# Spreading U of units 4 to 7 by TensorE, and calling for half of w1 and w2 three steps later

## The chip, the cores and the metric

The kernel runs on one core of a Trainium2 chip. The core has five engines that run beside each other and wait for one another by semaphores: TensorE (PE, matmuls; its weight loads are listed as PEld), VectorE (DVE), ScalarE (ACT), GpSimd (POOL) and SyncE (SP), which here only issues transfers. Sixteen DMA engines move data between HBM and the on-chip memory. The metric is device time in microseconds (us), the median of several executions; lower is better.

## The reference

The program computes an mLSTM cell over 4 batches, 8 heads, 768 positions and head size 40, and feeds the result to a multiplicative feed-forward block. Cut to what matters:

```python
for t in range(S):
    m_new = np.maximum(f_gate[:, :, t] + m, i_gate[:, :, t])
    f_stab = np.exp(f_gate[:, :, t] + m - m_new)
    i_stab = np.exp(i_gate[:, :, t] - m_new)
    C = f_stab * C + i_stab * outer(v_t, k_t)          # per batch and head
    n = f_stab * n + i_stab * k_t
    y[:, :, t] = sigmoid(o_gate_t) * (C @ q_t) / max(|n . q_t|, 1)
# (B, H, S, D) -> (B*S, H*D), 3072 tokens of 320
a = x @ w1                    # 320 x 1024
b = x @ w2                    # 320 x 1024
out = ((a * b) @ w3) @ w_out  # 1024 x 1024, 1024 x 320
```

The weights arrive as 64-bit floats. The kernel loads their words as 32-bit integers and makes 32-bit floats of them on the chip.

## The kernel before

The recurrence over time is done in blocks. A unit is 128 positions of one batch with all 8 heads; there are 24 units (6 blocks of positions by 4 batches), unit n being block `c = n // 4` of batch `b = n % 4`. One step s of the main loop finishes unit s - 1 and begins unit s, and does some matmuls of the feed-forward block beside it. The weight of one position in another is the exponential of a sum of two terms. One of them, U, is the same for all source positions, so the row of U that belongs to a head has to be spread over 64 partitions. For units 0 to 3 TensorE does that: a column of the identity matrix, broadcast, picks the row. For all later units U was written to HBM at the start and is read back with a broadcast over partitions, two transfers of 128 KB a unit.

```python
B, L, P, NU = 4, 64, 128, 24            # batches, half unit, unit, units
...
def load_u(n):                           # U of unit n from HBM, broadcast over 64 partitions
    c, b = divmod(n, B)
    src = U_d[2 * c:2 * c + 2, b * H:(b + 1) * H, :].rearrange("x h t -> x (h t)")
    for x in range(2):
        nc.sync.dma_start(out=weights_tile(n)[halves[x]].rearrange("p h t -> p (h t)"),
                          in_=src[x:x + 1].to_broadcast([L, H * L]))
...
def spread(n):                           # U of unit n by TensorE, into one PSUM bank
    ub = mps([P, H, L], "ub")
    for h in range(H):
        r = n % B * H + h
        for x in range(2):
            mm(ub[halves[x], h, :], ident[0:RG, r:r + 1].to_broadcast([RG, L]), U[:, x * L:(x + 1) * L])
    return ub

def weights(n):
    c, b = divmod(n, B)
    src = weights_tile(n) if c else spread(n)
    pw = weights_tile(n)
    for h in range(H):
        nc.scalar.activation(out=pw[:, h, :], in_=src[:, h, :], func=AF.Exp, bias=aT[:, c, b * H + h:b * H + h + 1])
    for r in halves:                     # the causal mask, on GpSimd
        nc.gpsimd.affine_select(out=pw[r], in_=pw[r], compare_op=OP.is_ge, fill=0.0, base=0,
                                pattern=[[0, H], [1, L]], channel_multiplier=-1)

def turn(n):                             # k and q of units 0 to 9 transposed by TensorE
    ...
    for src, dst, name in ((kbuf[n % NB], kT_t, "kT"), (qbuf[n % NBQ], qT_t, "qT")):
        pt = mps([128, NP, P], "pt")
        for p in range(NP):
            transpose(pt[:, p, :], src[:, 2 * p:2 * p + 2, :].rearrange("p a b -> p (a b)"))
        dst[n] = sb.tile([128, NP, P], FP, name=name, tag=name)
        nc.scalar.copy(out=dst[n], in_=pt)

def weighted(n):                         # vw: v times the input weight, on GpSimd
    ...
```

`mps` hands out one of four PSUM banks, which the transposes (pt, px), U (ub) and the up-products (pa, pb) share in the first part of the kernel. [...]

A weight tile goes through three hands: `fetch` issues its transfer (a tile of w1 or w2 is 128 rows of 4 KB, 512 KB), `scale_next` scales its two words on ScalarE, and `convert` puts them together on VectorE. The tiles of w1 and w2 are called w0 to w9 here: w0 to w4 hold the first half of the columns (the fifth tile the rest of the rows, in both), w5 to w9 the second half. Then come eight tiles of w_out and sixteen of w3. The first transfers, and the plan by steps:

```python
load(0, slice(0, 2))                     # k and q of unit 0
fetch("w12", 0, 0)
load(0, slice(2, 3))                     # v
fetch("w12", 1, 0)
load_o(0)
fetch("w12", 2, 0)
idle += [w3o_words[:, i * CW:(i + 1) * CW] for i in range(2)]
fetch("w12", 3, 0)
fetch("w12", 4, 0)
load(1)                                  # k, q, v of unit 1
load_o(1)
...                                      # the gates' scans on DVE, then
turn(0)
gate_cols(a, aT, nc.scalar.copy)
scale_next(True)                         # w0
scale_next(True)                         # w1
convert()
nc.scalar.activation(out=w, in_=w, func=AF.Exp)
weights(0)
...
scale_next(True)                         # w2
convert()
...
todo = w12[KF * 2 + 1:] + [("wo", ...)] + [("w3", ...)]
n_cvt = [2, 1, 1, 1, 2, 2, 3, 3, 3] + [2] * 7    # conversions in each step
turned, converted, fetched = 0, 2, 2 * KF + 1    # KF is 2

for s in range(len(n_up)):
    if B <= s + 3 < NU:
        load_u(s + 3)
    if s + 2 < NU:
        load(s + 2); load_o(s + 2)
    if 0 < s < B - 1:
        weights(s + 1); out_gate(s)
    if s < NU:
        weighted(s)
        ...
        if 0 < s < N_DVE:
            turn(s)
    ...                                  # x_trans (px): y of an earlier unit turned for the feed-forward
    now = [ups.pop(0) for _ in range(n_up[s])]   # n_up: 1 in steps 4 and 5, 2 in steps 6 to 16
    open_ups = [up(*x) for x in now]     # pa, pb
    ...                                  # up_rest, then the cell: unit s-1 finished, unit s begun (ss, pc)
    if s == 0:
        gate_cols(g, gT, nc.scalar.copy); out_gate(0); scale_next(); weights(1)
    if B - 1 <= s < NU:
        weights(s + 1); out_gate(s)
    for _ in range(n_cvt[s]):
        convert(); converted += 1        # scales first if nothing is scaled
    ...
    while todo and fetched < converted + (2 if s < 2 else 3 if s < ahead - 1 else 4):
        fetch(*todo.pop(0)); fetched += 1
```

The second half of the columns of w1 and w2 is first used by the up-products of step 7.

Of the kernel before, what the change touches and what calls it, by code (L numbers as in the profile page):

```python
# [16 lines left out]
def kernel(  # L17
# [28 lines left out]
    B, H, S, D = q.shape  # L46
    L = 64
    P = 128
    NT = S // L
    NT2 = S // P  # L50
    NU = NT2 * B
# [6 lines left out]
    FO = DFF // P  # L58
    KF = DM // P
# [17 lines left out]
    def mps(shape, name):  # L77
        pool = banks.pop(0)
        banks.append(pool)
        return pool.tile(shape, FP, name=name, tag="m")  # L80
# [10 lines left out]
    def mm(out, lhsT, rhs, start=True, stop=True):  # L91
        in_order(nc.tensor.matmul(out, lhsT=lhsT, rhs=rhs, start=start, stop=stop))  # L92
# [4 lines left out]
    halves = [slice(0, L), slice(L, P)]  # L97
# [3 lines left out]

    NB, NBQ = 4, 3
    N_DVE = 10
    q_all = const.tile([P, NBQ * H * DP], FP, name="q_all")
    qbuf = [q_all[:, i * H * DP:(i + 1) * H * DP].rearrange("p (h d) -> p h d", d=DP) for i in range(NBQ)]
    kbuf = [const.tile([P, H, DP], FP, name=f"kbuf{i}") for i in range(NB)]
    vbuf = [const.tile([P, H, D1], FP, name=f"vbuf{i}") for i in range(NB)]
    ident = const.tile([P, P], FP, name="ident")
# [16 lines left out]
    def load(n, which=slice(0, 3)):  # L125
        for dst, src in ((kbuf[n % NB][:, :, 0:D], k), (qbuf[n % NBQ][:, :, 0:D], q), (vbuf[n % NB][:, :, 0:D], v))[which]:
            if src is not q or n < N_DVE:
                nc.sync.dma_start(out=dst, in_=rows(src, n))  # L128
# [11 lines left out]
    def load_o(n):  # L140
        o_t[n] = io.tile([P, H, D], FP, name="o_in", tag="o_in", bufs=4)
        nc.sync.dma_start(out=o_t[n], in_=rows(o_gate, n))
# [8 lines left out]
    def weights_tile(n):  # L151
        if n not in u_t:
            u_t[n] = io.tile([P, H, L], FP, name="pw", tag="pw", bufs=5)
        return u_t[n]
# [45 lines left out]
    def fetch(kind, i, part):  # L200

        if kind == "w12":
            c0 = part * CW
            if i < 2 * KF:
                wt, src = ((w1, w1_d), (w2, w2_d))[i // KF]
                ko = i % KF
                dst, pieces = wt[:, ko, c0:c0 + CW], [(every, src[ko * 128:(ko + 1) * 128, cols(c0, CW)])]
            else:
                dst, pieces = wr[:, c0:c0 + CW], [(slice(j * REM, (j + 1) * REM), src[KF * P:DM, cols(c0, CW)])
                                                  for j, src in enumerate((w1_d, w2_d))]  # L210
        elif kind == "wo":
            dst, pieces = wo[:, i, :], [(square, wo_d[j * CQ + i * 32:j * CQ + (i + 1) * 32, :])
                                        for j, square in enumerate(squares)]
        else:
            dst, pieces = None, [(square, w3_d[i * 128 + part * 64:i * 128 + (part + 1) * 64, cols(j * CQ, CQ)]
                                  .rearrange("(m r) n -> r m n", m=2)) for j, square in enumerate(squares)]
        pend.append((dst, raw_tile(dst.shape[-1] if dst is not None else CW, pieces), i, part))
# [5 lines left out]
    def scale_next(early=False):  # L223
        scaled.append(pend.pop(0))
        scale(scaled[-1][1], early)
# [36 lines left out]
    def spread(n):  # L262


        ub = mps([P, H, L], "ub")
        for h in range(H):
            r = n % B * H + h
            for x in range(2):
                mm(ub[halves[x], h, :], ident[0:RG, r:r + 1].to_broadcast([RG, L]), U[:, x * L:(x + 1) * L])
        return ub  # L270

    def weights(n):
        c, b = divmod(n, B)
        src = weights_tile(n) if c else spread(n)
        pw = weights_tile(n)
        for h in range(H):
            nc.scalar.activation(out=pw[:, h, :], in_=src[:, h, :], func=AF.Exp, bias=aT[:, c, b * H + h:b * H + h + 1])  # L277
        for r in halves:
            nc.gpsimd.affine_select(out=pw[r], in_=pw[r], compare_op=OP.is_ge, fill=0.0, base=0,  # L279
                                    pattern=[[0, H], [1, L]], channel_multiplier=-1)  # L280
# [161 lines left out]
    RG = GR * BH  # L442
# [19 lines left out]
    load(0, slice(0, 2))  # L462
    fetch("w12", 0, 0)
    load(0, slice(2, 3))
    fetch("w12", 1, 0)
    load_o(0)
    fetch("w12", 2, 0)
    idle += [w3o_words[:, i * CW:(i + 1) * CW] for i in range(2)]
    fetch("w12", 3, 0)
    fetch("w12", 4, 0)  # L470
    load(1)
    load_o(1)

    nc.vector.memset(on, 1.0)
    nc.vector.memset(on.rearrange("p (c t) -> p c t", t=L)[:, :, 0:1], 0.0)
# [221 lines left out]
    n_seven = [0] * 19 + [1] * 12 + [0]  # L697
    n_down = [0] * 17 + [2] * 6 + [1] * 7 + [0, 5]
    w12 = [("w12", i, part) for part in range(2) for i in range(2 * KF + 1)]
    todo = w12[KF * 2 + 1:] + [("wo", i, 0) for i in range(FO)] + [("w3", ko, part) for ko in range(FO) for part in range(2)]  # L700
    n_cvt = [2, 1, 1, 1, 2, 2, 3, 3, 3] + [2] * 7
    pinned, ahead = 32, 9
    behind = ExitStack()
    turned, converted, fetched = 0, 2, 2 * KF + 1

    for s in range(len(n_up)):
        if B <= s + 3 < NU:
            load_u(s + 3)
        if s + 2 < NU:
            load(s + 2)  # L710
            load_o(s + 2)
        if 0 < s < B - 1:
            weights(s + 1)
            out_gate(s)
        if s < NU:
            weighted(s)
            if s >= B:
                decayed(state[s % B][1], state[s % B][0], s, 0)
            if 0 < s < N_DVE:
                turn(s)  # L720
        if NY <= s - 2 < NU:
            send(s - 2)
        elif 0 <= s - 2 < NY:
            twice(s - 2)
        if NY <= s - 2 < NU:
            get_back(s - 2)
        while turned < min(s - 2, NY):
            x_trans(turned)
            turned += 1
        fold()  # L730
        seven = None
        if n_seven[s]:
            seven = up_by_seven(*sevens.pop(0), (lambda i: cell[i // 2][:, i % 2].rearrange("p (i t) -> p i t", i=2)) if s <= NU else
                                lambda i: mps([128, 2, TH], "p67" if i < 2 else "p15"))
            if s <= NU:
                seven[0]()
            seven[1]()
        if seven and s <= NU:
            ffn_out([downs.pop(0) for _ in range(n_down[s])], [cell[1][:, i, 0:DM] for i in range(2)])
        else:  # L740
            for _ in range(n_down[s]):
                ffn_out([downs.pop(0)])
        if seven and s > NU:
            seven[0]()
        now = [ups.pop(0) for _ in range(n_up[s])]
        open_ups = [up(*x) for x in now]
        if len(now) == 1 and turned == s - 2 < NY:
            x_trans(turned)
            turned += 1

        def rest():
            for x in open_ups:
                up_rest(*x)
            if seven:
                seven[2]()

        gated = None
        if s <= NU:
            gated = quarter_work(s, rest)
        else:  # L760
            rest()
        with tc.issue_after(gated.ins) if gated else nullcontext():
            if seven:
                seven[3]()
            if NY <= s - 2 < NU:
                x_turn(s - 2)
            if N_DVE <= s + 1 < NU:
                gated = turn(s + 1)
            if s in (16, 17):
                weight_sums(s - 16)  # L770
            if s - 2 in range(4 * GT - 1, NU, GT):
                token_sums((s - 2) // GT)
        if s == 0:
            gate_cols(g, gT, nc.scalar.copy)
            out_gate(0)
            scale_next()
            weights(1)
        if s == NU:
            cell_psum.close()
            banks.extend([ps_m] * 3 + [ctx.enter_context(tc.tile_pool(name="ps_x", bufs=4, space=bass.MemoryType.PSUM))] * 4)  # L780
        if B - 1 <= s < NU:
            if s + 1 < NU:
                weights(s + 1)
            out_gate(s)
        with tc.issue_after(gated.ins) if N_DVE <= s + 1 < NU else nullcontext():
            for _ in range(n_cvt[s] if s < len(n_cvt) else 0):
                convert()
                converted += 1
        if s >= ahead:
            while pend and len(scaled) < 2:  # L790
                scale_next()
        if N_DVE <= s + 2 < NU:
            load_turned(s + 2)
        while todo and fetched < converted + (2 if s < 2 else 3 if s < ahead - 1 else 4):
            fetch(*todo.pop(0))
            fetched += 1
        if s + 1 == pinned:
            for ins in keep_order(front):
                behind.enter_context(tc.issue_after(ins))
# [30 lines left out]
```

## Time and profile before

| what | value |
|---|---|
| median time of 3 runs | 447.19 us (446.38 to 449.67) |
| span of the profiled execution | 445.8 us |
| PE busy | 423.7 us, 95% of the span |
| PEld busy | 335.5 us, 75% |
| DVE busy | 306.3 us, 69% |
| ACT busy | 149.3 us, 34% |
| POOL busy | 81.7 us, 18% |
| moved by the DMA engines | 52.72 MB, mean 118 GB/s |
| transfers of U (pw<-U_d) | 40 of 128 KB, 3.7 us from issue to landing |

The page of the profile cuts the span into 40 slices of about 11 us; one digit is the busy share of an engine in a slice in tenths, and the line PEclk is the clock that TensorE was granted, in tenths of full speed. Groups of instructions are named by line, engine, operation, and the tiles written and read, as `pw<-U_d`. An answer of the timeline starts with the start and the length of an instruction or a merged row of them, and ends in brackets with the idle time before it and what ended that. A wait for several semaphores is put down to the one that came last.

### The profile page before, as it was taken

The numbers are of one execution on the slowest core, as the hardware profiler recorded it, in microseconds if no ns is written. First come the engines' busy times: TensorE is split into PE (matmuls) and PEld (weight loads), VectorE is DVE, ScalarE is ACT, GpSimd is POOL, SyncE is SP. The second block draws the span as 40 slices with busy tenths as digits, with TensorE's granted clock in tenths as the row PEclk, the third lists the DMA queues.
The fourth block names the chain that finished last, engine by engine and source line by source line (L and its number), as shares of the span: only waits on it lengthen the run. The fifth ranks groups of instructions, "written<-read, shape, count | busy, mean of one in ns | idle before, by whom it ended". The sixth has DMA issues, their size and how long they took to land.

```text
span 445.8 us, 12871 instructions
## 1 busy us (share of the span) xinstructions
PE 423.7 (95%) x5271; PEld 335.5 (75%) x5271; DVE 306.3 (69%) x639; ACT 149.3 (34%) x407; POOL 81.7 (18%) x154
## 2 busy tenths in 40 slices
PE   4768989898999999999999999999999999999997
PEld 3656877787878878787877877778778777777774
DVE  5578387668866976696677949668699776444800
ACT  3766465445752454253212321213211111101110
POOL 3344043233211220222022203202020000000000
PEclk9995899999999999999999999999999999999999
DMA  8999989778988798697366466364111120000001
GB/s 203 182 175 201 200 142 170 172 176 166 205 198 186 147 180 177 161 165 140 83 116 148 102 132 140 76 136 109 50 35 35 39 46 16 15 16 15 1 30 44
DMA packets 136555, 52.72 MB, mean 118 GB/s; under 512 B 109936, under 2 KB 127536, under 8 KB 136496
## 3 DMA queue, kind: packets, MB, share of 16 engines
q1 hardware_dynamic: 132896, 47.87, 53.7%
q10 hardware_dynamic: 3600, 4.03, 2.7%
q8 instruction: 41, 0.67, 0.7%
q14 instruction: 18, 0.15, 0.1%
HBM read 46.07 MB, written 5.80 MB: 116 GB/s over the span
## 4 chain that ended last, share of the span: by engine, by line
PE 80%; DMA 5%; SPq 5%; ACT 3%; DVE 2%; POOL 2%; issue 2%; DVEq 0%; POOLq 0%
PE cell L92 22%; PE pa L92 18%; PE po L92 14%; PE pb L92 12%; PE wp L92 8%; PE p L92 5%; SPq L173 2%; SPq L128 2%; DMA raw<-in_moe_w_dram 2%; DMA o_in<-in_o_gate_dram 1%; DMA kbuf<-in_k_dram 1%; PE px L95 1%; POOL pw L279 1%; ACT pw L277 1%; ACT raw L180 1%
## 5 line engine op out<-in xcount | busy, mean ns | idle before, releaser
L92 PE MATMUL pa<-xT,w 128*128 128x256 f32 x240 | 62.1, 391 | 0.6 <-ACT xT L437 0.6
L92 PE MATMUL po<-w3o,ab 128*128 128x320 f32 x224 | 61.8, 433 | 0.0
L92 PEld LDWEIGHTS po<-w3o,ab 128*128 128x128 f32 x224 | 42.4, 190 | 17.3 <-issue 0.4
L306 POOL TENSOR_TENSOR state<-state,decay 128x164 f32<-128x164 f32 x40 | 19.7, 492 | 182.5 <-DVE den L387 168.2
L92 PEld LDWEIGHTS pa<-xT,w 128*128 128x128 f32 x240 | 45.7, 195 | 8.5 <-ACT xT L437 1.0
L92 PE MATMUL pb<-xT,w 128*128 128x256 f32 x192 | 45.9, 382 | 2.3 <-ACT kT L296 2.3
L583 DVE TENSOR_TENSOR ab<-pb,a_sb 128x512 f32<-128x512 f32 x24 | 16.6, 692 | 43.6 <-ACT a_sb L582 43.6
L279 POOL TENSOR_SCALAR_AFFINE_SELECT pw<-pw 64x512 f32<-64x512 f32 x48 | 34.4, 717 | 52.9 <-ACT pw L277 48.3
L92 PE MATMUL cell<-w3o,ab 128*128 128x320 f32 x160 | 44.0, 432 | 0.0
L92 PEld LDWEIGHTS pb<-xT,w 128*128 128x128 f32 x192 | 36.7, 192 | 8.2 <-ACT kT L296 3.1
L277 ACT ACTIVATE pw<-pw,aT 128x64 f32<-128x64 f32 x160 | 40.2, 336 | 2.8 <-ACT o_sb L685 2.8
L582 ACT ACTIVATE a_sb<-pa 128x512 f32<-128x512 f32 x24 | 14.3, 598 | 76.3 <-PE pb L92 76.3
L92 PEld LDWEIGHTS cell<-w3o,ab 128*128 128x128 f32 x160 | 30.4, 190 | 12.0
L630 DVE SCALAR_TENSOR_TENSOR a_sb<-pa,wo 128x512 f32<-128x512 f32 x12 | 8.3, 692 | 43.2 <-PE pa L92 43.2
L92 PE MATMUL pa<-xT,wr 64*64 64x256 f32 x384 | 36.8, 386 | 0.0
L92 PE MATMUL pb<-xT,wr 64*64 64x256 f32 x384 | 36.2, 379 | 0.0
L92 PE MATMUL wp<-wo,w3T 128*128 128x320 f32 x128 | 35.8, 432 | 0.0
L379 DVE TENSOR_TENSOR h<-cell,h 64x164 f32<-64x164 f32 x96 | 31.3, 326 | 1.8
L92 PEld LDWEIGHTS wp<-wo,w3T 128*128 128x128 f32 x128 | 23.7, 190 | 8.9
L92 PEld LDWEIGHTS pa<-xT,wr 64*64 64x64 f32 x384 | 19.0, 132 | 14.4 <-issue 8.4
L685 ACT COPY o_sb<-po 128x320 f32<-128x320 f32 x14 | 6.0, 427 | 67.4 <-PE po L92 67.4
L92 PEld LDWEIGHTS pb<-xT,wr 64*64 64x64 f32 x384 | 20.2, 133 | 3.0
(128 smaller groups left out, 722.8 us busy)
## 6 DMA issues: line engine op xcount, KB each, us to landing
raw<-in_moe_w_dram SPq DMA_DIRECT2D x64, 128.0 KB, 3.4
pw<-U_d SPq DMA_DIRECT2D x40, 128.0 KB, 3.7
kbuf<-in_k_dram SPq DMA_DIRECT2D x24, 160.0 KB, 4.5
vbuf<-in_v_dram SPq DMA_DIRECT2D x24, 160.0 KB, 5.1
o_in<-in_o_gate_dram SPq DMA_DIRECT2D x24, 160.0 KB, 4.8
out_dram<-o_sb ACTq DMA_DIRECT2D x24, 160.0 KB, 1.8
raw<-in_moe_w_dram SPq DMA_DIRECT2D x7, 512.0 KB, 5.6
raw<-in_moe_w_out_dram SPq DMA_DIRECT2D x32, 80.0 KB, 2.3
```

Source lines behind the costliest of these rows:

```text
L92: in_order(nc.tensor.matmul(out, lhsT=lhsT, rhs=rhs, start=start, stop=stop))
L95: in_order(nc.tensor.transpose(out, in_, ident[0:n, 0:n]))
L128: nc.sync.dma_start(out=dst, in_=rows(src, n))
L173: nc.sync.dma_start(out=dst, in_=src)
L277: nc.scalar.activation(out=pw[:, h, :], in_=src[:, h, :], func=AF.Exp, bias=aT[:, c, b * H + h:b * H + h + 1])
L279: nc.gpsimd.affine_select(out=pw[r], in_=pw[r], compare_op=OP.is_ge, fill=0.0, base=0, pattern=[[0, H], [1, L]], channel_multiplier=-1)
L306: nc.gpsimd.tensor_tensor(out=new, in0=old, op=OP.mult, in1=decay[:, b * NP:(b + 1) * NP, 2 * c + x:2 * c + x + 1] .to_broadcast([P, NP, D1]))
L379: nc.vector.tensor_tensor(out=part, in0=ph[x][halves[e]], in1=part, op=OP.add)
L582: nc.scalar.mul(out=a_sb, in_=pa, mul=UP ** -2)
L583: nc.vector.tensor_tensor(out=ab_t[gr][j][:, fs[0]:fs[-1] + 1, t0:t0 + a_sb.shape[-1]], in0=pb, in1=a_sb, op=OP.mult)
L630: nc.vector.scalar_tensor_tensor(out=out, in0=p, scalar=UP ** -2, in1=q, op0=OP.mult, op1=OP.add)
L685: nc.scalar.copy(out=o_sb, in_=po)
```

## The change

Two things are changed.

- Units 4 to 7, the second block of positions, get U by TensorE as units 0 to 3 do, so 8 transfers of 128 KB are no longer needed. `spread` takes the block's columns of U, which stay on the chip until step 8.
- Of w1 and w2 only three tiles are called for before the main loop. The last two of the first half follow in steps 0 and 1, and the second half in steps 3 to 5, where before it was steps 0 to 4. Conversions move accordingly: 1, 1, 1, 0 in the first four steps where there were 2, 1, 1, 1, and 4 in each of steps 7 and 8 where there were 3. The rows of k, q, v and o of the second unit are called for between the first tiles of words.

The aim is to take transfers out of the first part of the kernel, in which the DMA engines are busy nearly all the time, and to have the rows of the next units arrive sooner.

```diff
+    N_PE = 8
     def spread(n):
+        c, b = divmod(n, B)
         ub = mps([P, H, L], "ub")
         for h in range(H):
-            r = n % B * H + h
+            r = b * H + h
             for x in range(2):
-                mm(ub[halves[x], h, :], ident[...], U[:, x * L:(x + 1) * L])
+                mm(ub[halves[x], h, :], ident[...], U[:, c * P + x * L:c * P + (x + 1) * L])
     def weights(n):
-        src = weights_tile(n) if c else spread(n)
+        src = weights_tile(n) if n >= N_PE else spread(n)
     load(0, slice(0, 2))
     fetch("w12", 0, 0)
     load(0, slice(2, 3))
+    load(1, slice(0, 2))
     fetch("w12", 1, 0)
     load_o(0)
+    load(1, slice(2, 3))
     fetch("w12", 2, 0)
+    load_o(1)
     idle += [w3o_words[:, i * CW:(i + 1) * CW] for i in range(2)]
-    fetch("w12", 3, 0)
-    fetch("w12", 4, 0)
-    load(1)
-    load_o(1)
-    todo = w12[KF * 2 + 1:] + [("wo", ...)] + [("w3", ...)]
-    n_cvt = [2, 1, 1, 1, 2, 2, 3, 3, 3] + [2] * 7
+    todo = w12[3:] + [("wo", ...)] + [("w3", ...)]
+    n_cvt = [1, 1, 1, 0, 2, 2, 3, 4, 4] + [2] * 7
+    n_fetch = [4, 5, 5, 7, 9, 12, 16, 20]
-    turned, converted, fetched = 0, 2, 2 * KF + 1
+    turned, converted, fetched = 0, 2, 3
     for s in range(len(n_up)):
-        if B <= s + 3 < NU:
+        if N_PE <= s + 3 < NU:
             load_u(s + 3)
...
         if s == 0:
             gate_cols(g, gT, nc.scalar.copy)
             out_gate(0)
-            scale_next()
             weights(1)
...
-        while todo and fetched < converted + (2 if s < 2 else 3 if s < ahead - 1 else 4):
+        while todo and fetched < (n_fetch[s] if s < len(n_fetch) else converted + 4):
             fetch(*todo.pop(0))
             fetched += 1
```

Cuts are marked by three dots; line numbers move by one or two.

More of the change, by code (lines that the diff above doesn't have):

```diff
@@ L262, in spread @@
     def spread(n):
+        c, b = divmod(n, B)
         ub = mps([P, H, L], "ub")
         for h in range(H):
-            r = n % B * H + h
+            r = b * H + h
             for x in range(2):
-                mm(ub[halves[x], h, :], ident[0:RG, r:r + 1].to_broadcast([RG, L]), U[:, x * L:(x + 1) * L])
+                mm(ub[halves[x], h, :], ident[0:RG, r:r + 1].to_broadcast([RG, L]), U[:, c * P + x * L:c * P + (x + 1) * L])
         return ub
@@ L699 @@
     w12 = [("w12", i, part) for part in range(2) for i in range(2 * KF + 1)]
-    todo = w12[KF * 2 + 1:] + [("wo", i, 0) for i in range(FO)] + [("w3", ko, part) for ko in range(FO) for part in range(2)]
-    n_cvt = [2, 1, 1, 1, 2, 2, 3, 3, 3] + [2] * 7
+    todo = w12[3:] + [("wo", i, 0) for i in range(FO)] + [("w3", ko, part) for ko in range(FO) for part in range(2)]
+    n_cvt = [1, 1, 1, 0, 2, 2, 3, 4, 4] + [2] * 7
+    n_fetch = [4, 5, 5, 7, 9, 12, 16, 20]
     pinned, ahead = 32, 9
     behind = ExitStack()
-    turned, converted, fetched = 0, 2, 2 * KF + 1
+    turned, converted, fetched = 0, 2, 3
     for s in range(len(n_up)):
-        if B <= s + 3 < NU:
+        if N_PE <= s + 3 < NU:
             load_u(s + 3)
```

## The prediction

> **What bounds the kernel now.** I read the page first: the slices of the span, then the share of each engine. TensorE (PE) is at nine tenths or more from the sixth slice on, and the DMA engines at eight tenths or more through the first nine slices, so two different limits follow each other.
>
> ```profile
> PE   4768989898999999999999999999999999999997
> ...
> PEclk9995899999999999999999999999999999999999
> DMA  8999989778988798697366466364111120000001
> ```
>
> What comes after about 60 us is a full queue on PE: a microsecond lost or added before that point, or added to PE anywhere, stays in the time. So I asked for the busy time by stretches.
>
> ```profile
> 11.00:13.00 2.00, 1.65 (x34) 1.23 (x34) 0.69 (x1) 2.00 (x12) 0.03 (x1) 1.00 0.99 369
> 15.00:19.00 4.00, 3.66 (x74) 3.36 (x76) 2.56 (x6) 1.95 (x6) 0.75 (x2) 1.00 1.19 131
> 31.00:48.00 17.00, 14.46 (x192) 11.89 (x192) 11.41 (x27) 6.79 (x17) 6.04 (x11) 0.51 1.07 198
> 60.00:123.00 63.00, 59.81 (x991) 50.34 (x984) 47.82 (x105) 36.83 (x98) 18.24 (x30) 1.00 0.84 173
> ```
>
> The last three columns are granted clock, DMA share and GB/s. From 11 to 13 us weight words arrive at 369 GB/s; from 15 to 19 us rows of k, q, v, o arrive at 131 GB/s with the DMA engines just as busy. From 31 to 48 us PE is busy for 14.46 of 17 us at half clock: about 7 us lost to the clock. From 60 us on PE has 3.2 us of gaps in 63.
>
> Then the waits in the first 60 us: how often does PE, or ScalarE (ACT), really wait for a transfer?
>
> ```profile
> PE pt L95 <- DMA kbuf<-in_k_dram: 7.3, 3, 5.6
> ...
> ACT raw L180 <- DMA raw<-in_moe_w_dram: 1.0, 1, 1.0
> ```
>
> Three waits for k: 5.6 us is the very first; the other two, 0.77 and 0.88 us, are steps 3 and 4. No engine has a wait for U. Last, the order in time:
>
> ```profile
> 10.23 0.70 ACT L180 ACTIVATE raw<-raw 128x512 f32<-128x512 f32 x1 [0.95 <-DMA raw<-in_moe_w_dram]
> 10.84 0.40 ACT L542 ACTIVATE gates<-gates 96x256 f32<-96x256 f32 x1
> 11.14 1.69 ACT L277 ACTIVATE pw<-ub,aT 128x64 f32<-128x64 f32 x8
> ...
> 16.88 3.68 PE L92 MATMUL ub<-gates,ident 96*64 96x64 f32 x64
> ...
> 25.26 1.15 PE L92 MATMUL ub<-gates,ident 96*64 96x64 f32 x32
> ...
> 32.94 1.08 PE L95 MATMUL pt<-ident,kbuf 128*128 128x128 f32 x4 [0.77 <-DMA kbuf<-in_k_dram]
> ...
> 40.58 1.09 PE L95 MATMUL pt<-ident,kbuf 128*128 128x128 f32 x4 [0.88 <-DMA kbuf<-in_k_dram]
> ...
> 78.28 1.99 PE L92 MATMUL pb<-xT,w 128*128 128x256 f32 x8 [0.82 <-ACT kT L296]
> ```
>
> Read here: [...]the exponentials of unit 0 stand behind the scaling of the second weight tile, which waited for its words. Unit 1's rows never kept PE waiting: its transpose starts at 20.49 us, when the 64 ub matmuls end. And from step 7 on, a matmul (pb) can wait for ACT to empty the transpose tile (kT) whose PSUM bank it takes.
>
> [...]
>
> **The start: words behind rows.** The order of issue was k0, q0, w0, v0, w1, o0, w2, w3, w4, then unit 1. It becomes k0, q0, w0, v0, k1, q1, w1, o0, v1, w2, o1. A row load is 164 KB; at 131 GB/s that is 1.25 us. The tile w1, which ACT waits for until 10.23 us, now has k1 and q1 ahead: 2 x 1.25 = 2.5 us later, about 12.7 us. Everything behind it on ACT slides: exponentials of unit 0, the mask, vw(0), the products pc(0) at 15.34 us, the ub matmuls. One scaling (0.66 + 0.67 us) leaves step 0, but the exponentials at 18.90 us waited for ub(1), which ended only about 18.7, so it returns 0.2. Steps 0 to 2 are chains ACT, POOL, PE of about 6 us with no transfer in them: **+2.3 us**.
>
> **What the lighter DMA stream gives back.** Up to k3 the stream loses w4 and w5, each 0.52 MB at 369 GB/s = 1.4 us, and U of unit 4 (0.26 MB, at least 0.7 us): k3 comes 3.5 us earlier or better, and PE comes 2.3 us later. Both waits, 0.77 and 0.88 us, vanish. **-1.65 us.** That is all the transfers can return, for no other wait of PE was theirs.
>
> **U by TensorE.** Eight transfers of 128 KB fall away and 4 x 32 matmuls come; the recorded order has each set of 32 behind pc(s), in steps 3 to 6, ahead of the next transposes. At full clock 1.15 us each, 4.6 us in all; the first perhaps at half clock, 1.97. More than that: before, ACT could start the 8 exponentials right after a_sb, while PE did the cell products. Now they wait for ub, and kT, which frees a bank, comes after the exponentials and the scalings. I assigned the banks from the built program: ub takes one of the four, and pa of step s+1 (pb in step 5) waits for the exponentials. Counting from the end of pc:
> - Step 4: ub 1.97, 8 exponentials 1.75, out gate 0.36, kT and qT 1.06, xT 0.5, so pa starts 5.8 us after pc(3), where it was 4.35: **+1.45**.
> - Step 5: before, px waited for y from POOL, so PE had 2 us of slack. POOL's mask is now 0.4 us later: **+0.4**.
> - Step 6: PE needs ub 1.12, transposes 0.93, pa 1.73, pb 1.73 = 5.5, but the second pa waits for kT at 1.2 + 1.75 + 0.36 + two scalings 2.25 + 0.56 = 6.1. Then 2 x 1.73: 9.6 against 7.85 before: **+1.75**.
> - Step 7: pa waits for the exponentials (0.6), pb for kT, at 3.3 + scalings 1.13 + 2 x 0.78 + 0.56 = 6.55; then 3 x 1.73: 11.8 against 9.3: **+2.5**.
>
> **Conversions moved back.** Steps 7 and 8 convert four tiles in place of three: one scaling pair of 0.78 us more on ACT ahead of kT in steps 8 and 9. Step 8 had 0.26 us of slack, step 9 already a wait of 1.50 us: +0.5 and +0.8, **+1.3**.
>
> Sum: 2.3 - 1.65 + 1.45 + 0.4 + 1.75 + 2.5 + 1.3 = **+8.0 us** with the clock as it was; from 447.2, **455.2**.
>
> **Rivals.** (1) *The clock stays up.* The transfers no longer hold steps 3 and 4[...]. If PE does not fall to half clock at 31 us[...] up to 7 us of the slow stretch come back: 448 to 449. [...]Against it: the drop follows step 2, where PE waits for ACT and POOL (0.86, 1.04 and 0.84 us), and the change leaves those waits alone. I give it a third. (2) *The DMA engines are the real bound* of the first 60 us (share above 1), and 1.05 MB less, with 1 MB postponed, moves all of it forward: 5 us or more gained, 441 to 444. For it: the chain of waits runs through issues and transfers of k and raw. Against it: PE's own waits there sum to 1.65 us, and the cell steps 0 to 2 are chains on ACT. One in ten. (3) *ACT becomes the bound* of steps 4 to 7 more than I reckon, since [...]each wait starts from PE: another 2 to 4 us, 457 to 459. (4) The words come too late for step 7, which first uses the second half: their last tile is called for in step 5 and needed at the end of step 6, some 10 us, against a landing of 3.4 us; I count it out.
>
> **Range and chances.** 455.2 in the main case, 448.5 in a third of the cases, 442 in a tenth: weighted about 452 to 453. I put it at **452.9 us**, eight in ten between **446.0** and **458.5**. Faster by over 2% (below 438.2) 0.03; slower by over 2% (above 456.1) 0.19; within, 0.78.
>
> **What would show it.** Right, if in the profile after: ACT's second scaling starts at 12 to 13 us with a wait of about 3 us for raw; PE's waits for kbuf are the first one alone; ub stands at 128 more matmuls, 4.6 us or a little more; pa waits for ACT pw and pb for ACT kT between 60 and 95 us, some 4 us in sum; the window 31 to 48 us still shows a clock near half. Wrong, if the second scaling is not late (the start then costs nothing), if the clock never falls to half after 30 us, or if PE reaches its full queue several microseconds before it did.

## The result, and the profile after

The changed kernel takes 460.75 us (median of 4, 459.55 to 461.74), the kernel before 447.75 in the same comparison: ratio 1.029 (1.024 to 1.034). Ratios, here and below, leave out executions more than 1.5% above the fastest of their kernel. The profiled spans are 445.8 and 457.8 us. The prediction was 452.9, with 446.0 to 458.5; its main case, 455.2, is 5.5 us short as well.

The slices of the profile after, the counterparts of those shown of before:

```profile
PE   4588889889899999999999999999999999999997
...
PEclk9997799999999999999999999999999999999999
DMA  8998931766997877897635574564121220000001
```

TensorE (PE) reaches its full queue later, its slow stretch is shorter, and the transfers, at seven tenths or more through sixteen slices before, have a hole at the sixth and seventh. The same stretches as before:

```profile
11.00:13.00 2.00, 0.25 (x2) 0.00 (x0) 0.00 (x0) 0.00 (x0) 0.00 (x0) 1.00 0.96 257
15.00:19.00 4.00, 1.69 (x46) 1.27 (x49) 1.94 (x4) 2.73 (x12) 2.10 (x3) 1.00 1.09 232
31.00:48.00 17.00, 13.75 (x322) 11.99 (x323) 13.99 (x34) 7.90 (x23) 7.64 (x13) 0.77 0.89 160
60.00:123.00 63.00, 56.14 (x904) 46.51 (x906) 42.81 (x91) 34.96 (x95) 18.66 (x29) 1.00 0.60 131
```

At 11 to 13 us PE is now busy for 0.25 of 2 us: ScalarE (ACT) waits for words until its second scaling, which before started at 10.23 us:

```profile
13.69 0.69 ACT L181 ACTIVATE raw<-raw 128x512 f32<-128x512 f32 x1 [3.99 <-DMA raw<-in_moe_w_dram]
```

From 31 to 48 us the mean clock is 0.77, not 0.51. From 60 to 123 us PE has 6.9 us of gaps, not 3.2. What it waits for in the first 60 us (us in total, times, the longest):

```profile
PE pt L95 <- DMA kbuf<-in_k_dram: 5.6, 1, 5.6
...
PE ub L92 <- issue: 2.7, 1, 2.7
PE pt L95 <- issue: 1.3, 1, 1.3
PE cell L92 <- issue: 1.1, 2, 0.9
```

Of the three waits for k only the first is left, as predicted. New are 5.1 us of "issue": PE waited for nothing that the profile shows. And from 60 to 140 us:

```profile
PE pb L92 <- ACT kT L298: 5.3, 3, 2.3
PE pa L92 <- ACT xT L439: 0.7, 1, 0.7
PE pa L92 <- ACT pw L279: 0.6, 1, 0.6
```

Before, the waits of pb for kT were 2.3 us in the whole span:

```profile
L92 PE MATMUL pb<-xT,w 128*128 128x256 f32 x192 | 45.9, 382 | 2.3 <-ACT kT L296 2.3
```

To see in which step time goes, I take from the timeline where the cell of each unit starts (its first `cell<-qT,kT` row) and subtract the kernel before. The columns behind the first are runs told of below; each column is one execution. In microseconds:

| start of the cell of unit | after | U alone | U alone, early | words alone | rows first | after, U early |
|---|---|---|---|---|---|---|
| 0 | 3.44 | 0.34 | 0.25 | 3.26 | 2.65 | 2.85 |
| 2 | 3.37 | 0.58 | 0.48 | 3.14 | 3.77 | 2.77 |
| 4 | 2.30 | 0.82 | -0.05 | -0.95 | 1.43 | -3.39 |
| 5 | 5.24 | 2.68 | -0.80 | -0.94 | 1.44 | -3.19 |
| 6 | 7.08 | 4.15 | 0.48 | 0.24 | 1.45 | -1.25 |
| 7 | 9.63 | 6.37 | -0.61 | 0.59 | 1.44 | -2.34 |
| 9 | 11.08 | 6.29 | -0.56 | 2.14 | 1.35 | -0.65 |
| 11 | 12.05 | 6.29 | -0.56 | 4.19 | 1.36 | -0.31 |

In the first column the difference stays the same after unit 11 to the end. So the changed kernel loses 3.4 us at the start, gets 1.1 back by unit 4, loses 7.3 in steps 5 to 7 (the U of units 5 to 7) and 2.4 in steps 8 to 10.

Step 5 holds what no part of the prediction foresaw. PE's timeline of the changed kernel:

```profile
54.69 0.63 PE L92 MATMUL cell<-vw,kbuf 64*64 64x41 f32 x32
55.25 0.92 PE L92 MATMUL ub<-gates,ident 96*64 96x64 f32 x24
58.91 0.45 PE L92 MATMUL ub<-gates,ident 96*64 96x64 f32 x8 [2.74 <-issue]
```

In the middle of 32 like matmuls, with operands long in place, PE stops for 2.74 us. My theory from here: it waits for its own *instructions*. PE's stream has 5399 matmul records, a weight load for each and 78 others, some 10,900 in all; the page lists a queue for instructions with 42 packets of 16 KB, one for about 259 of them. Counted so, the gap stands at record 1730; those at 31.01, 34.79 and 40.13 us at 708, 963 and 1218. The distances, 255, 255 and 512, are multiples of 256 to within one. From here on I add 62 to the count, which puts the four gaps at 1792 (7 x 256), 768, 1024 and 1280; that 62 instructions without a record stand ahead is not shown, and the argument needs only the common remainder. The queues from 55 to 56 us (packets, MB, share of 16 engines):

```profile
q1 hardware_dynamic: 790, 0.13, 123.7%
q8 instruction: 1, 0.02, 9.7%
```

One block came in just then, between 790 packets of the other queue; 9.7% of 16 engine-microseconds is 1.55 us for its own transfer. It landed at 57.38 us, and PE went on at 58.91. PE had passed the multiple before, 1536, at about 53.6 us, ran the 256 instructions of cell and ub behind it in 2.6 us, and stood until 5.3 us had gone by.

### The profile page after: what moved, and what is told of

It reads as the page before. It is cut to its first block, busy times and chain, and to the rows that moved or that the text cites. A ratio compares the mean times of both kernels' runs of the same rounds, so it can differ in the third digit from the quotient of the medians.

```text
span 457.8 us, 13117 instructions
## 1 busy us (share of the span) xinstructions
PE 427.8 (93%) x5399; PEld 338.7 (74%) x5399; DVE 306.8 (67%) x639; ACT 148.3 (32%) x407; POOL 80.9 (18%) x154
## 4 chain that ended last, share of the span: by engine, by line
PE 79%; ACT 7%; DMA 5%; SPq 2%; DVE 2%; issue 2%; POOL 0%; ACTq 0%; DVEq 0%
PE cell L92 21%; PE pa L92 19%; PE po L92 13%; PE pb L92 12%; PE wp L92 7%; PE p L92 5%; DMA raw<-in_moe_w_dram 3%; ACT pw L279 2%; DMA q_all<-in_q_dram 2%; ACT raw L185 2%; PE ub L92 1%; ACT raw L181 1%; SPq L129 1%; SPq L174 1%; PE px L95 1%
## 5 line engine op out<-in xcount | busy, mean ns | idle before, releaser
L279 ACT ACTIVATE pw<-pw,aT 128x64 f32<-128x64 f32 x128 | 32.2, 336 | 2.8 <-ACT o_sb L686 2.8
L181 ACT ACTIVATE raw<-raw 128x512 f32<-128x512 f32 (+1 forms) x32 | 20.4, 636 | 7.8 <-DMA raw<-in_moe_w_dram 7.3
```

The source lines that it names most:

```text
L181: nc.scalar.activation(out=hi, in_=hi, func=AF.Prelu, scale=2.0 ** -111, alpha=2.0 ** 32)
```

## The experiments

Theory: the loss is U's, by where its work stands (the chain ub, exponentials, scalings, kT on ACT, and a run of cheap instructions that outpaces their fetch), plus the start, plus the late conversions. Rivals: the start; the clock; late transfers; the gap an accident. Times are medians of all executions; ratios, against the kernel before on the same chip (447.45 to 447.66), come with a 95% interval; the trace of run 10 is of an execution of 554.82 us and isn't read.

**1. U alone.** The kernel before with

```
+    N_PE = 8                                  # as in the change, and its spread()
...
-        src = weights_tile(n) if c else spread(n)
+        src = weights_tile(n) if n >= N_PE else spread(n)
...
-        if B <= s + 3 < NU:                   # fetch U from unit 4
+        if N_PE <= s + 3 < NU:
```

> The kernel before with only the U of units 4 to 7 made by TensorE; order of the transfers, scalings and conversions as before. Reading of the traces: the whole change lost 13.0 us, of which U owns the later ub work of steps 4 to 7 (about 1.1 us in step 4 or 5, 1.9 in step 6 or 7) and the gap of 2.74 us inside ub(5), which lies on the 1792nd instruction of TensorE's stream (7 x 256). Here that instruction falls on ub(5) too, so: 5 to 6 us slower than before, 452.5 to 454, with an issue gap of 2 us or more in ub(5). Rival A (the gap is an accident of one run, or belongs to the late start): 2 to 3.5 us slower, no gap in ub(5). Rival B (the recorded sum, steps 4 to 7 at 6.1 us and no gap): 6 us slower, spread over the pa and pb waits, no gap.

Measured: 454.59 us, 1.017 (1.013 to 1.021), 7 us lost, a little more than expected. The gap is there at 1792, but with 1.62 us, not 2 or more. The table shows the rest: 1.9, 1.5 and 2.2 us in steps 5, 6 and 7, nothing after. Rival A is out; of rival B the waits are there, but not without a gap.

**2. Words alone.** The changed kernel with `N_PE = 4`.

> The changed kernel with the U of units 4 to 7 fetched again as before; rows ahead of words and later conversions stay. Reading: start +3.35 us, less what the k waits and a shorter half-clock stretch give back (about -1), conversions moved back +3 in steps 9 to 11: 4.5 to 6 us slower than before, 452 to 453.5, so that this run and the run with U alone add up to the whole loss of 13. Rival A (the two parts only hurt together, because U's work meets the late conversions on ScalarE): under 3 us slower. Rival B (start alone, the conversions absorbed): 2 to 2.5 us slower.

Measured: 450.23 us, 1.006 (1.004 to 1.009), 2.7 us lost: less than I expected, and in the range of rival A. The table shows 3.3 at the start, all of it and more got back by unit 4, then 1.6 in step 8 to 9 and 2.0 in step 10. Runs 1 and 2 sum to 9.7 of 13 us; some of the loss needs both parts.

**3. The start put back.** The changed kernel with

```
     load(0, slice(2, 3))
-    load(1, slice(0, 2))
     fetch("w12", 1, 0)
     load_o(0)
-    load(1, slice(2, 3))
     fetch("w12", 2, 0)
+    load(1)
     load_o(1)
```

> The changed kernel with one thing put back: the words of the second and third weight tile ahead of the second unit's rows, as in the kernel before (the fourth and fifth tile stay later). Reading: ScalarE's second scaling starts near 10.2 us again, the transposes of unit 1 near 20.5, and of the 3.35 us most stays in the time: 2.4 to 3.4 us faster than the changed kernel, 457.3 to 458.4. Rival A (the late start is made up by step 4, because rows of k then come earlier): under 1 us faster than the changed kernel, 460 to 461. Rival B (the drop of the clock moves with the start): the half-clock stretch gets longer by 2 us or more and the time comes back by 1 us or less.

Measured: 457.68 us, 1.023 (1.020 to 1.027), 3.1 us faster than the changed kernel. This looked like the value of the start; run 9 shows that it isn't in general. The gap at 1792 is longer here:

```profile
56.07 0.70 PE L92 MATMUL ub<-gates,ident 96*64 96x64 f32 x8 [4.02 <-issue]
```

**4. The changed kernel, shifted.** Ahead of the first transposes, where PE only waits for k:

```
+    for i in range(30):
+        mm(cell[0][0:32, 0, 0:1], ident[:, 0:32], ident[:, 0:1])
```

> The changed kernel with 30 tiny matmuls (32 columns of weights, one moving column) at the head of TensorE's stream, where it only waits for the first k: some 120 instructions more, so every later 256th instruction falls 120 earlier in the program. If the gaps are fetches of TensorE's own instructions in blocks of 256: the 2.74 us gap in ub(5) goes; 2048 then falls on the products of unit 5's cell and 2304 on ub(6), where a new, shorter gap of 0 to 2 us may open; 1 to 2.7 us faster than the changed kernel, 458 to 459.7. Rival (the gap belongs to ub(5) itself: its operands, its bank, or a missing record): the gap stays in ub(5) with 2 us or more, and the time is that of the changed kernel, 460 to 461.5.

Measured: 465.17 us, 1.040 (1.035 to 1.045), 4.4 us *slower* than the changed kernel. The gap left ub(5) and stood where the count says, at 2304, in ub(6):

```profile
62.10 0.68 PE L92 MATMUL ub<-gates,ident 96*64 96x64 f32 x16
64.64 1.12 PE L92 MATMUL ub<-gates,ident 96*64 96x64 f32 x16 [1.86 <-issue]
```

with others at 1024, 2816, 4864 and 6144 (0.93, 0.61, 1.53, 1.73 us). Place: as the theory has it. Without its gap, step 5 is 0.2 us longer than before, where the changed kernel has 2.9. Time: wrong; a cell and its ub are 320 cheap instructions, so at many alignments a block of 256 lies wholly within them, and I had moved one out of step 5 and others into steps 6, 7, 12 and 15. Nor are the gaps all of it: step 9 has none and is 4.9 us longer than before (changed kernel 0.8), with a wait of pb for kT of 3.34 us and 6.8 us at half clock behind it. After the gap in ub(6) the clock fell too, and pa took 3.60 us where it takes 1.89; the windows of that run show the stretch:

```profile
64.20:71.00 6.80, 6.36 (x33) 5.52 (x34) 4.37 (x11) 5.13 (x15) 3.62 (x6) 0.51 0.07 17
```

**5. The kernel before, shifted**, by the same 30 matmuls.

> The kernel before with the same 30 tiny matmuls at the head of TensorE's stream. Control for the shifted run of the changed kernel, which was 4.4 us slower than the changed kernel although its gap in ub(5) was gone: new gaps of 1.86 us in ub(6), 0.61, 1.53 and 1.73 us at the new multiples of 256, and half-clock stretches behind two of them. If the gaps are instruction fetches: here too the gaps stand at the new multiples of 256 (1280, 1792, 2048, 2304 lie in cells of units 3, 4, 5, 6), the gap of 0.87 us in pc(7) goes, and the time moves by up to 3 us either way, 446 to 451. Rival A (the tiny matmuls themselves delay the first transposes): pt(0) starts later than 5.6 us by as much as the time grows. Rival B (gaps have nothing to do with the place in the stream): the 0.87 us gap stays in pc(7), time within 0.5 us of before.

Measured: 451.99 us, 1.011 (1.008 to 1.014). The 0.87 us gap in pc(7) is gone; new ones stand at 1024 (0.23 us), 4608 and 5888:

```profile
145.17 0.32 PE L92 MATMUL cell<-vw,kbuf 64*64 64x41 f32 x7 [1.47 <-issue]
...
193.49 0.31 PE L92 MATMUL cell<-vw,kbuf 64*64 64x41 f32 x3 [1.73 <-issue]
```

The tiny matmuls end before the first transposes start, at 5.47 us. So the place of the same work in the stream is worth up to 4.5 us here. Over the 15 traces other than that of run 10, the 47 PE gaps that the timeline gives to "issue" all stand at the same place in a block of 256, within two instructions. And the instruction queue shows what each waited for: its packets come in the order of the blocks, and in all 47 cases the packet of the block that PE stood before landed 1.2 to 1.8 us (median 1.46) before PE went on.

**6. U alone, early.** Run 1, with the work of U moved:

```
+        if B - 1 <= s < N_PE - 1:     # right behind turn(s) and x_trans,
+            weights(s + 1)            # ahead of the up products
         fold()
...
-            if s + 1 < NU:            # behind the cell
+            if N_PE <= s + 1 < NU:
                 weights(s + 1)
```

> The kernel with U alone, where the ub matmuls and the exponentials of units 4 to 7 stand right behind the step's transposes, ahead of the up products, in place of behind the cell. U alone took 7 us more than before. If its loss is (a) ScalarE's chain ub, exponentials, scalings, kT at the end of steps 3 to 6 and (b) instruction gaps because cell and ub made one run of 320 cheap instructions: both go, the pb waits for kT fall to the 0.8 and 1.5 us of before, and 4 to 6 us come back, 448.5 to 450.5. Rival A (the loss is TensorE's 4.6 us of ub work itself, which no order hides): at most 2 us back, 452.5 or more. Rival B (early exponentials hold up the copies of xT, and so pa): slower than U alone.

Measured: 444.56 us, 0.994 (0.992 to 0.996): 10 us better than run 1 and 3 us better than before. PE's timeline in step 5 of this kernel, then ACT's:

```profile
53.39 0.60 PE L95 MATMUL pt<-ident,q_all 128*128 128x128 f32 x4
53.92 1.15 PE L92 MATMUL ub<-gates,ident 96*64 96x64 f32 x32
55.00 1.99 PE L92 MATMUL pa<-xT,w 128*128 128x256 f32 x8
```

```profile
54.28 0.59 ACT L298 COPY kT<-pt 128x512 f32<-128x512 f32 x1
54.74 0.60 ACT L298 COPY qT<-pt 128x512 f32<-128x512 f32 x1
55.22 1.76 ACT L279 ACTIVATE pw<-ub,aT 128x64 f32<-128x64 f32 x8
```

The exponentials run while PE does pa and pb, which it would do anyway, and kT is copied first. In the changed kernel ACT's timeline of step 6 has the other order:

```profile
69.14 1.74 ACT L279 ACTIVATE pw<-ub,aT 128x64 f32<-128x64 f32 x8 [2.38 <-PE ub L92]
...
73.33 0.62 ACT L298 COPY kT<-pt 128x512 f32<-128x512 f32 x1
```

ACT is idle 2.38 us for ub, then kT comes 4.2 us behind it. With ub early the waits of pb for kT are 1.5 us in all (before: 2.3; U alone: 3.5). Rival A, that the ub matmuls themselves are the loss, is out: this kernel has all of them. The gaps don't explain it by their sum, which is 4.3 us here and 3.05 in run 1, but the one in step 5 is gone. Of the 10 us the two traces, of one execution each, show 6.9: 2.6 in step 5, 0.2 in step 6, 3.3 in step 7 and 0.9 before unit 4.

**7. Later calls alone.** Run 2 with the start of run 3 and

```
-    n_cvt = [1, 1, 1, 0, 2, 2, 3, 4, 4] + [2] * 7
-    n_fetch = [4, 5, 5, 7, 9, 12, 16, 20]
+    n_cvt = [1, 1, 1, 0, 2, 3, 3, 3, 3, 3] + [2] * 6
+    n_fetch = [4, 5, 5, 7, 10, 13, 16, 19]
```

> The changed kernel with U of units 4 to 7 fetched again and the words of the second and third tile back ahead of the second unit's rows, so that of the change only the later calls for the second half remain; conversions 3 in steps 5 to 9 in place of 2, 2, 3, 4, 4. From the runs: rows ahead of words cost 3.1 to 3.4 us at the start, which go; words alone stood 2.7 us above before in the median. Expected: start as before (second scaling near 10.2 us), steps 9 to 11 lose less than the 3.5 us that words alone lost there, 446 to 448.5, level with before or 1 us better. Rival A (late conversions lose as much in any distribution): 449 or more. Rival B (the lighter stream keeps the clock up, fewer than the five half-clock windows of 3.4 us that before had): 443 to 446.

Measured: 449.02 us, 1.003 (1.001 to 1.005). No gain from calling later: rival A. Its trace is ahead by 4.5 us at unit 4 and gives it all back by unit 11; ACT waits for raw up to 1.9 us and PE 2.09 us for xT behind it.

**8. Conversions 3 in steps 7 to 10** of the changed kernel.

```
-    n_cvt = [1, 1, 1, 0, 2, 2, 3, 4, 4] + [2] * 7
-    n_fetch = [4, 5, 5, 7, 9, 12, 16, 20]
+    n_cvt = [1, 1, 1, 0, 2, 2, 3, 3, 3, 3, 3] + [2] * 5
+    n_fetch = [4, 5, 5, 7, 9, 12, 15, 18]
```

> The changed kernel with 3 conversions in steps 7 to 10 in place of 4, 4, 2, 2. The trace of the changed kernel has pb waiting for kT 1.47, 1.57 and 2.29 us in steps 7, 8 and 9, and 0.7 us for xT behind it; from step 7 to step 10 it loses 5.0 us against before. If the fourth conversion's scalings on ScalarE ahead of kT make these waits: steps 8 and 9 give 0.8 us each back, step 10 may give 0.5 away: about 1 to 1.5 us faster, 459.2 to 459.8. Rival A (the waits belong to transfers of words that land late: ScalarE waits for raw, 1.8 us before step 10): no change, 460.3 to 461.2. Rival B (spread out, they only hit more steps): slower by up to 1 us.

Measured: 458.62 us, 1.026 (1.022 to 1.030), 2.1 us faster than the changed kernel, but not by what was changed: at unit 7 it is already 2.5 us ahead, though its program is that of the changed kernel up to step 6. So two executions of the same instructions lie up to 4.0 us apart in these traces (at unit 4), and differences of that size at the start of one trace prove little. From unit 7 to unit 12 it loses 2.8 us, where the changed kernel loses 2.4. The pb waits fell to 0.81 and 0.83 us as expected; waits of 1.98 and 1.06 us for xT came, behind ACT's waits for raw. The cost moved: with the conversions spread, the transfers of rival A set the end.

**9. Rows first.** The kernel before, with the order of the start alone:

```
     load(0, slice(2, 3))
+    load(1, slice(0, 2))
     fetch("w12", 1, 0)
     load_o(0)
+    load(1, slice(2, 3))
     fetch("w12", 2, 0)
+    load_o(1)
...
     fetch("w12", 3, 0)
     fetch("w12", 4, 0)
-    load(1)
-    load_o(1)
```

> The kernel before with only the start's order changed as in the changed kernel: rows of the second unit ahead of the words of the second and third weight tile (fourth and fifth tile behind them, as early as they can); U, scalings, conversions and later calls as before. The recorded sum took 2.3 us for this (two row loads of 1.25 us, 0.2 made up); the trace of the changed kernel had 3.4 us at cell 0 to cell 2. If the rows cost what they take on the queue: second scaling 3 to 3.5 us later than 10.23, and 2.5 to 3.4 us slower, 450 to 451. Rival A (earlier k3 and k4 rows make it up by step 4): within 1 us of before. Rival B (clock: fewer half-clock windows behind the late start): level or up to 2 us faster.

Measured: 447.68 us, 1.000 (0.999 to 1.002). The second scaling is 2.7 us late, at 12.90 us; at unit 3 the trace is 4.2 us behind, with a gap of 3.02 us at 1024; at unit 4 it is 1.4 behind, and in the median nothing is left. That fits the ranges of both rivals, and both show: the two later waits for k are gone (rival A), and two stretches are at half clock, 3.4 us each, where before it was 17 us (rival B); which of them made up the start is not shown.

```profile
37.00:40.40 3.40, 3.02 (x21) 2.71 (x21) 2.27 (x7) 0.97 (x2) 1.16 (x2) 0.51 1.05 141
...
47.00:50.50 3.50, 3.50 (x10) 2.83 (x10) 1.97 (x3) 0.00 (x0) 2.12 (x4) 0.54 0.76 100
```

**10. The changed kernel with U early**: the edit of run 6 on the changed kernel.

> The changed kernel with one thing moved: the ub matmuls, exponentials and mask of units 4 to 7 stand right behind the step's transposes, ahead of the up products. On the kernel with U alone this move gave 10 us back. If the place of ub is what U costs here too (the 2.74 us gap in ub(5), and the waits of pa and pb for ScalarE in steps 6 and 7, 1.8 and 2.5 us): the trace grows by about 0.5 us in step 5, and by under 0.5 in steps 6 and 7, and the time falls by 6 to 9 us, to 452 to 455; what stays above before is the start (3.4) and steps 8 to 10. Rival (in the changed kernel the late words hold ScalarE anyway, so U's place matters less): 2 to 4 us back, 457 to 459.

Measured: 448.60 us, 1.003 (1.001 to 1.005): 12 us back, more than I expected. Run 11 is the same kernel.

**11. The same, for its trace.**

> The changed kernel with ub of units 4 to 7 early, once more, for a trace that can be read step by step. If the place of ub was the cause: from the cell of unit 4 to the cell of unit 7 the step lengths are those of the kernel before (34.4 us in sum) or up to 1 us more, where the changed kernel took 41.8; no gap stands in ub(5); pa and pb of steps 6 and 7 don't wait for ScalarE beyond the 0.8 us that the kernel before has. What stays: the second scaling near 13.7 us, fewer half-clock windows than before, and 1 to 3 us over steps 8 to 10. Rival: the 12 us come from the start or from the clock (cell of unit 4 earlier by 5 us or more), and steps 5 to 7 still take 39 us or more.

Measured: 448.86 us, 1.000 (0.999 to 1.002). From the cell of unit 4 to that of unit 7: 35.5 us (before 34.4, changed 41.8). In this execution PE never falls to half clock after 26 us; others of the same kernel had mean clocks down to 0.98.

```profile
31.00:48.00 17.00, 15.12 (x409) 13.20 (x409) 12.32 (x31) 9.98 (x30) 8.83 (x15) 1.00 0.92 172
```

The 2.0 us over steps 8 to 10 stay. Steps 5 to 7 return 6.3 of the 12 us. At unit 4 this trace is 3.4 us *ahead* of before and 5.7 ahead of the changed kernel, as the rival had it; whether that is the clock, the place of the U of unit 4, or the spread between executions isn't separated.

**12. U alone, early, with 43 tiny matmuls**, each with 64 x 64 weights, meant to put the blocks better.

```
+    for i in range(43):
+        x, e = quarters[i % 4]
+        mm(cell[0][halves[e], x, 0:1], ident[halves[x], 0:L], ident[halves[x], 0:1])
```

> The kernel with U alone, ub early (444.6 us), with 43 tiny matmuls at the head of TensorE's stream (172 instructions), chosen from the traces so that few blocks of 256 instructions lie wholly in the cheap cell matmuls. Without them it had instruction gaps of 1.05, 2.03 and 0.92 us, and three half-clock windows of 3.4 us behind the second. If the gaps are fetches that take 3.5 to 6 us from the crossing of one multiple of 256 to the next: gaps sum to 1 to 3 us, and the time falls by 0.5 to 2.5 us, 442 to 444. Rival A (the half-clock windows come from the waits of the first 40 us anyway): within 0.5 us of 444.6. Rival B (other gaps open where the estimate has none): 445 to 447.

Measured: 445.19 us, 0.995 (0.993 to 0.997): nothing gained, and in the range of rival B. Gaps of 0.25, 2.10 and 1.02 us stand at 1024, 1536 and 2048.

**13. The kernel before with the same 43.**

> Control: the kernel before with the same 43 tiny matmuls. It has instruction gaps of 0.16 and 0.87 us; with the 172 instructions the estimate from its trace has about 1 us near 28 us and 0.6 near 75 us, that of 0.87 us gone: within 1 us of before, 446.5 to 448.5. 30 tiny matmuls gave 4.5 us more, with gaps of 1.47 and 1.73 us at 145 and 193 us. Rival A (tiny matmuls cost time at the start by themselves, 1 us or more): 448.5 to 451. Rival B (alignment matters more than the gaps say, by the half-clock windows behind them): 444 to 446.

Measured: 448.17 us, 1.000 (0.999 to 1.002), a gap of 1.12 us at 1024, none at 88 us: as expected, but for the gap near 75 us, which didn't come. The time differs from that of before by 0.5 us, so tiny matmuls cost little by themselves.

**14. U early for units 4 and 5 only**: run 6 with `N_PE = 6`.

> The kernel with U alone, ub early, for units 4 and 5 only; U of units 6 and 7 is fetched as before. If ub early still costs TensorE its 1.1 us a unit once the queue is full (steps 5 and 6): up to 2 us faster than with all four, 442.5 to 444. If the ub matmuls lie in waits that are there anyway, or the two transfers of 256 KB cost as much as they save: 444 to 446. If fewer transfers were what made U early faster than before (3 us): half of that goes, 445.5 to 447.

Measured: 449.66 us, 1.004 (1.001 to 1.006), 5 us worse than with all four, and outside all three expectations. It has 128 instructions fewer and gaps of 1.31, 1.14, 1.25 and 1.52 us, the last two at 4608 and 5888 as in run 5. They sum to 5.2 us, against 4.0 in the three large ones of run 6. The trace is 2.6 us ahead of before at unit 11 and loses 1.5 us at the gap at 4608 and 1.8 at that at 5888. So it doesn't answer what it was for: halving the work moved the blocks as well.

## Why the prediction missed

- **Start, +2.3.** Too small for the place where I reckoned it (3.4 at the cell of unit 0): the second scaling came 3.46 us later, not 2.5. As an entry in the sum it doesn't stand by itself: alone it costs 0.0 us in the median (run 9), and put back in the changed kernel it returns 3.1 (run 3).
- **Lighter stream, -1.65.** Both k waits are gone, as said. With step 4's +1.45 the terms up to unit 4 make 2.1; the trace has 2.3. (The parts written down for step 4 add to 5.64 us, not 5.8; pa started 5.45 us behind pc(3).) That agreement hides gaps of 1.26 and 0.89 us and a half-clock stretch 7 us shorter, none in the sum.
- **Step 5, "+0.4": the step that failed.** It has 2.94. I reckoned with the POOL mask and PE's slack, not with PE's own instruction stream; the gap in ub(5) is 2.74. With ub behind the cell, as reckoned, and no gap in ub(5), step 5 is 0.2 us longer than before (run 4), near the +0.4; where a gap of 1.62, 3.57 or 4.02 us stands (runs 1, 8 and 3), it is 1.9, 4.5 and 4.7 us longer.
- **Step 6, +1.75, and step 7, +2.5:** 1.84 and 2.55. The chain ub, exponentials, scalings, kT was read rightly: moved ahead of the up products, U's work costs 0.2 us in the two steps together in run 6, against 3.7 in run 1, and 0.85 in run 11, against 4.4 in the changed kernel.
- **Conversions, +0.5 and +0.8:** 0.68 and 0.77. The first is only that small because a gap of 0.87 us, which the kernel before has in the same step, is gone; the pb wait itself is 1.57.
- **Step 10, not in the sum:** 0.98. I counted late words out for step 7, rightly, and didn't follow the queue further: ACT waits 1.77 and 0.92 us for the raw words of w3, and pa 0.70 us for xT behind them. Runs 2, 7 and 8 lose time in the same way in steps 10 to 12.
- **Rival 1, a third for 448 to 449.** The clock did fall for 10.2 us only, not 17.1, and the time rose by 13. My "7 us lost to the clock", which took PE for the limit all through that stretch, isn't borne out either. Over 154 executions of the kernel before, those with mean clock 0.981 (0.019 x 2 x 446 = 17 us at half) had a median of 448.4, those with 0.992 (7 us at half) 447.7: 0.7 us for 10 us at half clock. A straight line through all 154 gives 1.0; the scatter is wide (446.6 at 0.988), and it is a correlation, not an experiment. The weights of the two rivals pulled the prediction from 455.2 to 452.9; the three cases as written give 451.7.
- **Rival 3, ScalarE more the bound:** the right direction, but steps 6 and 7 were as in the main case; what was missing was the gap of 2.74 us.
- **The slices.** In the lines shown the DMA engines are at eight tenths or more through seven slices, not nine, and PE stays at nine only from the eleventh, not the sixth.

The sum of 8.0 became 12.05 in the trace: 2.5 from step 5, 1.0 from step 10, 0.2 from the start to unit 4 and 0.3 from steps 6 to 9. What stays open: why U alone (7.0) and words alone (2.7) make 13 together; how the 12 us of run 10 divide between gap, chain, clock and the start; and why run 6 is faster than before.

## What to carry to other kernels

Moving work from a transfer to an idle-looking engine isn't judged by the work's own length but by its place in the order: the same 128 matmuls cost 7 us behind the cell and gained 3 ahead of the up products, where their followers on ScalarE had time; that move shifted the instruction gaps as well. Count the instructions of a stretch of tiny matmuls: in the changed kernel TensorE ran 256 of them in 2.6 us, the next block landed 3.8 us after the first of them, and TensorE stood for 2.74 us; 30 tiny matmuls ahead moved that gap from ub(5) to ub(6). A stretch at half clock needn't be a reserve that can be had back: run 9's trace has 10 us less of it than the kernel before, at the same median time.

## What the runs showed of the hardware

Stops of TensorE: the changed kernel's trace has 42 packets of 16 KB on the instruction queue. In the 15 traces 628 such blocks came in, and a gap stood before 47 of them, always at the same remainder of 256 within two instructions, and up to 4.02 us long. Where one stood, the way from the crossing of one multiple to the first instruction behind the next took 2.7 to 8.5 us. What sets off the transfer of a block isn't shown.

Half clock: the stretches after 26 us were 3.4 (run 9), 6.8 (run 4), 10.2 (changed kernel) and 17.1 us (kernel before), one, two, three and five times 3.4. Their sum differed from run to run of one kernel: mean clocks of 0.972 to 0.996 for the kernel before. What starts or ends such a stretch isn't shown.
